# Transposes of q, k and the channel MLP's input: from TensorE to DMA transposes issued by ScalarE

## The chip, the core and the metric

The kernel runs on one core of a Trainium2 chip. The core has a matrix engine (TensorE, PE in the profile), VectorE (DVE), ScalarE (ACT), GpSimd (POOL) and SyncE (SP), each with its own in-order queue of instructions, and sixteen DMA engines that all queues share. A DMA is issued by an engine's queue (SPq, ACTq, POOLq in the profile) and lands later. The metric is device time in microseconds (us), the median over runs.

## The reference: what is computed

Eight batches of causal windowed attention, eight heads of 64 over 576 positions, feed an MLP mixer. Cut to what matters:

```python
# q, k, v: (8 batches, 8 heads, 576 positions, 64), float32
scores = q @ k.T / 8            # heads 0-3: 0 <= pos_q - pos_k < 32
                                # heads 4-7: 0 <= rel < 128 and rel % 4 == 0
x  = softmax(masked scores) @ v                  # -> (8, 576, 512)
h  = relu(x^T @ w_tok1) @ w_tok2                 # token MLP: 576 -> 256 -> 576
u  = x + h^T
out = u + relu(u @ w_ch1) @ w_ch2                # channel MLP: 512 -> 1536 -> 512
```

A matmul on TensorE contracts over the partition dimension. The scores contract over the 64 head channels and the channel MLP's first product over the 512 channels, while q, k and u arise with positions on the partitions. So q, k and u each have to be transposed once per batch: 576 positions by 512 channels, three times, eight batches.

## The kernel before

The 576 positions are handled as five strips (s_i) of 128, 128, 128, 128 and 64. Everything between the float32 loads and the float32 result is float16.

One batch goes through these steps. `emit_loads_dma` issues fifteen loads (q, k, v by strip; 128 partitions of eight 256-byte pieces) from SP. `gen_casts` turns them to float16: q on ScalarE, k and v on VectorE. `gen_attention` first transposes q and k: for q, then k, for each pair of heads hp, five TensorE transposes fill one PSUM tile `tp` (two buffers), and one VectorE copy moves it to `qt` or `kt` in SBUF (L184 to L203). Then for each head, `emit_qk` runs five score matmuls, two Exps on ScalarE and the mask product on GpSimd or VectorE; `emit_av` follows two or three heads later with ten matmuls, a reciprocal and a scaling product on VectorE that writes `xn`. `gen_mixer` runs the token MLP (h1p: ten matmuls, two Relus on ScalarE; up: ten matmuls, five VectorE adds that write `u16`), transposes u (L250 to L269: for each of four channel blocks cb, five TensorE transposes into `tp` and one VectorE copy to `uT`), then the channel MLP: gp (96 matmuls of 288 columns, Relus half on ScalarE and half on VectorE, giving twelve `gt`), and yp (sixty matmuls of 512 columns, five VectorE adds, five stores issued from SP).

Three streams are interleaved by `drive`: in iteration `it` the attention of batch `it`, the mixer of batch `it`-1 and the casts of batch `it`+1. Each generator yields a cost (C_TP, C_QK and so on) and the stream that has least progress goes next. A tile framework then places the instructions on the engines' queues and adds the semaphore waits; it may set an instruction earlier or later than it was traced. Every buffer has a fixed number of copies (`bufs`), so a writer waits until the readers of the copy before are done.

Each DMA issued from SP or ACT signals one of eight completion semaphores (DMAHW0 to DMAHW7), used in turn; a DMA that takes a semaphore again first waits until the DMA that used it before has landed. In the kernel before, all 163 such DMAs are SP's. The weights are loaded from GpSimd's queue, cast on the way.

## Time and profile before

| | |
|---|---|
| median of 3 runs | 401.49 us (400.77 to 402.12) |
| span of the profiled execution | 403.1 us; no other time is given for that execution |
| PE busy | 356.7 us, 89% of the span, 2784 matmuls |
| DVE, ACT, POOL busy | 228.7, 137.5, 101.9 us |
| PE on L190 (transposes of q, k) | 320 instructions, 34.55 us busy |
| PE on L255 and L261 (transposes of u) | 128 and 32 instructions, 15.62 and 6.34 us busy |
| DVE copies L197, L201, L267 | 32 each; 13.55, 15.48, 14.31 us busy |
| mean granted TensorE clock | 0.962 of full |

Matmuls are pipelined, and each row's duration includes a fixed part that overlaps with the next matmul. What a matmul costs TensorE is therefore the distance from its start to the start of the next one, not its busy time. The busy time of ACT leaves out what its queue spends on issuing DMAs; those have rows of their own, with the engine named ACTq.

### The profile page before, as it was taken

The page shows a single profiled execution, that of the slowest core. Times are in us where ns is not written, and L with a number is a line of the kernel's source. Part 1 is how long each engine was busy: PE and PEld are TensorE (multiplying, and loading weights), DVE is VectorE, ACT ScalarE, POOL GpSimd, SP SyncE. Part 2 cuts the span into 40 slices and gives each one's busy share as a digit, 9 for nine tenths or more (in the row PEclk, how much of TensorE's full clock was granted, in tenths as well). Part 3 has the DMA queues.
Part 4 walks back from the last instruction along what each step waited for, and adds up shares of the span by engine and source line. Part 5 has one row for each costly group of instructions (what it writes and reads, how often), then busy time and mean ns, then how long its engine had stood idle before and what let it go on. Part 6 is the DMA issues. An engine that isn't in the chain of part 4 may idle for free.

```text
span 403.1 us, 6967 instructions
## 1 busy us (share of the span) xinstructions
PE 356.7 (89%) x2784; PEld 218.3 (54%) x2784; DVE 228.7 (57%) x550; ACT 137.5 (34%) x281; POOL 101.9 (25%) x69
## 2 busy tenths in 40 slices
PE   0487659997899989999899989998999989996995
PEld 0254337553575547655675557654764557553752
DVE  2487437755885496638754586448543574445432
ACT  2164024443174325422462236331443206321310
POOL 0044301541062404260063205140235106240000
PEclk9999869996899999999899999999999989999899
DMA  9999999349933789486961250020002100020002
GB/s 192 210 214 218 199 198 221 86 112 215 198 77 78 184 180 208 71 210 155 171 122 52 67 91 2 28 78 15 2 0 80 41 0 2 26 80 14 2 38 81
DMA packets 121473, 42.50 MB, mean 105 GB/s; under 512 B 113696, under 2 KB 116064, under 8 KB 121440
## 3 DMA queue, kind: packets, MB, share of 16 engines
q1 hardware_dynamic: 118192, 38.32, 46.3%
q0 software_dynamic: 3248, 3.74, 5.3%
q8 instruction: 22, 0.36, 0.4%
q14 instruction: 11, 0.09, 0.1%
HBM read 36.34 MB, written 9.44 MB: 114 GB/s over the span
## 4 chain that ended last, share of the span: by engine, by line
PE 75%; DVE 13%; DMA 7%; SPq 2%; ACT 1%; issue 1%; POOL 1%; POOLq 0%; ACTq 0%
DMA l_k_3_138<-in_k_dram 6%; SPq L105 2%; DMA l_q_4_83<-in_q_dram 1%; PE yp_4_4709 L293 1%; PE yp_4_4133 L293 1%; PE yp_4_2282 L293 1%; PE yp_4_1665 L293 1%; PE yp_4_3516 L293 1%; PE yp_4_2899 L293 1%; PE yp_3_4669 L293 1%; PE yp_3_4092 L293 1%; PE yp_3_3475 L293 1%; PE yp_3_2241 L293 1%; PE yp_2_918 L293 1%; PE yp_1_877 L293 1%
## 5 line engine op out<-in xcount | busy, mean ns | idle before, releaser
L276 PEld LDWEIGHTS <-w_2_340 128*128 128x128 f16 x192 | 19.5, 102 | 9.9 <-issue 4.7
L276 PEld LDWEIGHTS <-w_0_321 128*128 128x128 f16 x192 | 18.5, 99 | 7.3 <-DVE xn_1159 L179 0.3
L276 PEld LDWEIGHTS <-w_3_357 128*128 128x128 f16 x192 | 19.5, 101 | 5.3
L276 PEld LDWEIGHTS <-w_1_337 128*128 128x128 f16 x192 | 18.9, 101 | 4.2
L190 PE MATMUL tp_q_0_149<-ident,q_0_97 128*128 128x128 f16 (+1 forms) x5 | 1.4, 275 | 14.5 <-ACT q_0_97 L118 14.5
L190 PEld LDWEIGHTS <-q_0_97 128*128 128x128 f16 (+1 forms) x20 | 1.6, 117 | 16.6 <-ACT q_0_97 L118 15.6
L155 POOL TENSOR_TENSOR att_0_792<-att_0_792,mask_63 128x1024 f16<-128x1024 f16 x1 | 2.1, 2116 | 22.0 <-ACT att_0_792 L152 22.0
L155 POOL TENSOR_TENSOR att_0_2548<-att_0_2548,mask_63 128x1024 f16<-128x1024 f16 x1 | 2.1, 2128 | 20.5 <-ACT att_0_2548 L152 20.5
L155 POOL TENSOR_TENSOR att_0_4369<-att_0_4369,mask_63 128x1024 f16<-128x1024 f16 x1 | 2.1, 2120 | 20.5 <-ACT att_0_4369 L152 20.5
L155 POOL TENSOR_TENSOR att_0_1314<-att_0_1314,mask_63 128x1024 f16<-128x1024 f16 x1 | 2.1, 2122 | 19.6 <-ACT att_0_1314 L152 19.6
L155 POOL TENSOR_TENSOR att_0_3165<-att_0_3165,mask_63 128x1024 f16<-128x1024 f16 x1 | 2.1, 2128 | 19.1 <-ACT att_0_3165 L152 19.1
L155 POOL TENSOR_TENSOR att_0_3782<-att_0_3782,mask_63 128x1024 f16<-128x1024 f16 x1 | 2.1, 2124 | 19.1 <-ACT att_0_3782 L152 19.1
L155 POOL TENSOR_TENSOR att_0_1931<-att_0_1931,mask_63 128x1024 f16<-128x1024 f16 x1 | 2.1, 2123 | 19.1 <-ACT att_0_1931 L152 19.1
L346 POOL DMA_DIRECT2D w_0_235<-in_moe_w_tok_dram x1 | 0.7, 720 | 24.5 <-DVE w_1_238 L340 24.5
L237 PEld LDWEIGHTS <-w_0_290 128*128 128x128 f16 x40 | 4.0, 100 | 4.7 <-issue 0.8
L237 PEld LDWEIGHTS <-w_1_304 128*128 128x128 f16 x40 | 3.9, 97 | 3.9
L222 PEld LDWEIGHTS <-w_1_238 128*128 128x128 f16 x16 | 1.7, 105 | 5.9 <-issue 5.2
L276 PE MATMUL gp_0_0_600<-uT_2_589,w_2_340 128*128 128x288 f16 x1 | 0.4, 399 | 4.4 <-DVE uT_2_589 L267 4.4
L155 POOL TENSOR_TENSOR att_4_1535<-att_4_1535,mask_65 128x1024 f16<-128x1024 f16 x1 | 2.1, 2120 | 8.5 <-ACT att_4_1535 L152 8.5
L155 POOL TENSOR_TENSOR att_4_2769<-att_4_2769,mask_65 128x1024 f16<-128x1024 f16 x1 | 2.1, 2123 | 8.2 <-ACT att_4_2769 L152 8.2
L155 POOL TENSOR_TENSOR att_4_4003<-att_4_4003,mask_65 128x1024 f16<-128x1024 f16 x1 | 2.1, 2123 | 8.2 <-ACT att_4_4003 L152 8.2
L155 POOL TENSOR_TENSOR att_4_4585<-att_4_4585,mask_65 128x1024 f16<-128x1024 f16 x1 | 2.1, 2117 | 8.2 <-ACT att_4_4585 L152 8.2
(3217 smaller groups left out, 1288.7 us busy)
## 6 DMA issues: line engine op xcount, KB each, us to landing
w_0_321<-in_moe_w_ch_dram POOLq DMA_DIRECT2D x1, 384.0 KB, 7.8
w_1_337<-in_moe_w_ch_dram POOLq DMA_DIRECT2D x1, 384.0 KB, 9.0
w_2_340<-in_moe_w_ch_dram POOLq DMA_DIRECT2D x1, 384.0 KB, 10.1
w_3_357<-in_moe_w_ch_dram POOLq DMA_DIRECT2D x1, 384.0 KB, 11.1
mask_63<-att_masks SPq DMA_DIRECT2D x1, 256.0 KB, 2.5
mask_65<-att_masks SPq DMA_DIRECT2D x1, 256.0 KB, 3.2
l_q_0_67<-in_q_dram SPq DMA_DIRECT2D x1, 256.0 KB, 3.9
l_k_0_69<-in_k_dram SPq DMA_DIRECT2D x1, 256.0 KB, 4.6
```

What stands on the lines that cost most here:

```text
L105: nc.sync.dma_start(out=t32[0:ns], in_=src[b, :, s0:s0 + ns, :].rearrange("h s d -> s h d"))
L155: eng.tensor_tensor(out=att, in0=att, in1=m, op=ALU.mult)
L190: nc.tensor.transpose(out=pst[:, 128 * s_i:128 * s_i + ns], in_=src[0:ns, s_i, 2 * hp:2 * hp + 2, :].rearrange("s h d -> s (h d)"), identi ...
L222: nc.tensor.matmul(out=p, lhsT=w1[s_i][:, 128 * jb:128 * (jb + 1)], rhs=xnb[:, s_i].rearrange("s h d -> s (h d)"), start=(s_i == 0), stop= ...
L237: nc.tensor.matmul(out=p, lhsT=w2[jb][:, s0:s0 + 128], rhs=h1[jb], start=(jb == 0), stop=(jb == 1),)
L276: nc.tensor.matmul(out=p[:, 0:288], lhsT=w3[cb][:, 128 * mb:128 * (mb + 1)], rhs=uT[cb][:, 288 * sh:288 * (sh + 1)], start=(cb == 0), stop ...
L293: nc.tensor.matmul(out=p, lhsT=gt[mb][:, s0:s0 + 128], rhs=w4[mb], start=(mb == 0), stop=(mb == 11),)
L346: nc.gpsimd.dma_start(out=t, in_=moe_w_tok1[128 * s_i:128 * (s_i + 1), :])
```

## The change: what it does

The 480 transposes on TensorE and the 96 copies out of PSUM are taken out, with the identity matrix and its load. In their place stand 120 DMA transposes, 15 per batch, issued from ScalarE's queue: five for q, five for k and five for u, one per strip. Each reads a strip of up to 128 positions by 512 channels in SBUF and writes all four transposed blocks at once, into one tile per batch of 128 x 4 x 640 (q, k) or 128 x 4 x 576 (u), each with two copies. In the built program each is one instruction that cuts its source into tiles of 16 rows by 128 columns. The cost that `drive` counts for the transposes of one attention goes from eight to five C_TP; the mixer's yields come as one.

```diff
 def gen_attention(b):
-        for nm in ("q", "k"):
-            for hp in range(4):
-                pst = ps.tile([128, 1024], FP16, tag="tp", bufs=2, name=f"tp_{nm}_{b}_{hp}")
-                for s_i in range(NSB):
-                    ns = SB[s_i] if nm == "q" else 128
-                    src = q16 if nm == "q" else k16
-                    nc.tensor.transpose(
-                        out=pst[:, 128 * s_i:128 * s_i + ns],
-                        in_=src[0:ns, s_i, 2 * hp:2 * hp + 2, :].rearrange("s h d -> s (h d)"),
-                        identity=ident[0:ns, 0:ns],
-                    )
-                if nm == "q":
-                    qt = sb.tile([128, S], FP16, tag="qt", bufs=8, name=f"qt_{b}_{hp}")
-                    nc.vector.tensor_copy(out=qt, in_=pst[:, 0:S])
...
-                yield C_TP
+        qt = sb.tile([128, 4, KTW], FP16, tag="qt", bufs=2, name=f"qt_{b}")
+        kt = sb.tile([128, 4, KTW], FP16, tag="kt", bufs=2, name=f"kt_{b}")
+        for s_i in range(NSB):
+            ns = SB[s_i]
+            s0 = 128 * s_i
+            nc.scalar.dma_start_transpose(
+                out=qt[:, :, s0:s0 + ns],
+                in_=q16[0:ns, s_i].rearrange("s h d -> s (h d)"))
+            nc.scalar.dma_start_transpose(
+                out=kt[:, :, s0:s0 + 128],
+                in_=k16[:, s_i].rearrange("s h d -> s (h d)"))
+            yield C_TP
+        for hp in range(4):
+            qt_tiles[(b, hp)] = qt[:, hp]
+            kt_tiles[(b, hp)] = kt[:, hp]
 def gen_mixer(b):
-        uT = []
-        for cb in range(4):
-            pst = ps.tile([128, 1024], FP16, tag="tp", bufs=2, name=f"tpu_{b}_{cb}")
-            for s_i in range(NSB):
...
-            t = sb.tile([128, S], FP16, tag="ut", bufs=8, name=f"uT_{b}_{cb}")
-            nc.vector.tensor_copy(out=t, in_=pst[:, 0:S])
-            uT.append(t)
-            yield C_UT
+        uTt = sb.tile([128, 4, S], FP16, tag="ut", bufs=2, name=f"uT_{b}")
+        for s_i in range(NSB):
+            if s_i < 4:
+                nc.scalar.dma_start_transpose(out=uTt[:, :, 128 * s_i:128 * s_i + 128], in_=u16[s_i])
+            else:
+                nc.scalar.dma_start_transpose(out=uTt[:, :, 512:576], in_=u16[s_i][64:128])
+        yield 4 * C_UT
+        uT = [uTt[:, cb] for cb in range(4)]
...
-    nc.sync.dma_start(out=ident, in_=ident_dram)
...
-            n_att = 8 * C_TP + 8 * C_QK + 8 * C_AV
+            n_att = 5 * C_TP + 8 * C_QK + 8 * C_AV
```

Where the new instructions come to stand on ScalarE's queue is decided by the framework. Two places matter. In the rows below, names are the program's with the batch left out (att_7 is the masked score tile of head 7, h_4_0 the first half of the token MLP's hidden layer of batch 4, qt the transposed q), L numbers are lines of each kernel's own file, and the brackets name the semaphores that are waited for.

The first place is ScalarE's queue at the end of batch 4's attention. Before, the last Exp of head 7 is followed by the two Relus of the token MLP:

```order
L152 ACTIVATE att_7_2895<-scB_7_2889 128x512 [waits PE_49]
L229 ACTIVATE h_4_0_3000<-h1p_0_2994 128x512 [waits PE_49]
L229 ACTIVATE h_4_1_3008<-h1p_1_3002 128x512 [waits PE_49]
L118 CAST q_7_3912<-l_q_0_3581 128x512 [waits DMAHW3_49,PE_49]
L118 CAST q_7_3912<-l_q_1_3587 128x512 [waits DMAHW6_49]
L283 ACTIVATE gt_0_3124<-gp_0_0_3125 128x288 [waits PE_49]
```

Now ten transposes stand between them:

```order
L152 ACTIVATE att_7_2529<-scB_7_2523 128x512 [waits PE_49]
L189 DMA_TRANSPOSE qt_3184<-q_6_2862 128x4x128 [waits DMAHW4_49]
L192 DMA_TRANSPOSE kt_3185<-k_6_2863 128x4x128 [waits DMAHW5_49]
L189 DMA_TRANSPOSE qt_3184<-q_6_2862 128x4x128 [waits DMAHW7_49]
L192 DMA_TRANSPOSE kt_3185<-k_6_2863 128x4x128
L189 DMA_TRANSPOSE qt_3184<-q_6_2862 128x4x128 [waits DMAHW1_49]
L192 DMA_TRANSPOSE kt_3185<-k_6_2863 128x4x128 [waits DMAHW2_49]
L189 DMA_TRANSPOSE qt_3184<-q_6_2862 128x4x128 [waits DMAHW3_49]
L192 DMA_TRANSPOSE kt_3185<-k_6_2863 128x4x128 [waits DMAHW5_49]
L189 DMA_TRANSPOSE qt_3184<-q_6_2862 128x4x64 [waits DMAHW6_49]
L192 DMA_TRANSPOSE kt_3185<-k_6_2863 128x4x128 [waits DMAHW7_49]
L224 ACTIVATE h_4_0_2634<-h1p_0_2628 128x512 [waits PE_49]
```

They are batch 6's, which become possible when batch 4's scores have freed the tile's copy; batch 4's Relu is queued behind them. The same stands before the Relus of batches 3 (ten) and 5 (ten), and seven stand before batch 2's; before batch 0's stand four of batch 1, before batch 1's two, and before those of batches 6 and 7 none. The eighth of the ten takes the semaphore of the second again (DMAHW5), and the tenth that of the third (DMAHW7).

The second place follows on the same queue: from the token MLP's Relus to the first Relu of the channel MLP. The five transposes of u now stand there, each waiting for one VectorE add:

```order
L224 ACTIVATE h_4_1_2642<-h1p_1_2636 128x512 [waits PE_49]
L248 DMA_TRANSPOSE uT_2682<-u_4_0_2652 128x4x128 [waits DMAHW0_49,DVE_49]
L151 ACTIVATE att_0_2695<-scA_0_2688 128x512 [waits PE_49,Pool_49]
L248 DMA_TRANSPOSE uT_2682<-u_4_1_2659 128x4x128 [waits DMAHW1_49,DVE_49]
L248 DMA_TRANSPOSE uT_2682<-u_4_2_2666 128x4x128 [waits DMAHW2_49,DVE_49]
L248 DMA_TRANSPOSE uT_2682<-u_4_3_2671 128x4x128 [waits DMAHW3_49,DVE_49]
L152 ACTIVATE att_0_2695<-scB_0_2689 128x512 [waits PE_49]
L250 DMA_TRANSPOSE uT_2682<-u_4_4_2678 128x4x64 [waits DMAHW4_49,DVE_49]
L266 ACTIVATE gt_0_2699<-gp_0_0_2700 128x288 [waits PE_49]
```

On TensorE, what stood between up and the third block of gp was forty of the transposes; now only one head's scores stand there, and gp follows directly.

## The prediction

> **What bounds the kernel now.** I read the page's busy lines first, then busy time by stage, then the order of time in one steady batch.

> ```profile
> PE 356.7 (89%) x2784; PEld 218.3 (54%) x2784; DVE 228.7 (57%) x550; ACT 137.5 (34%) x281; POOL 101.9 (25%) x69
> PE 75%; DVE 13%; DMA 7%; SPq 2%; ACT 1%; issue 1%; POOL 1%; POOLq 0%; ACTq 0%
> 20.00:30.00 10.00, 8.45 (x69) 5.62 (x67) 8.35 (x37) 6.12 (x13) 4.70 (x9) 1.00 1.36 214
> 40.00:60.00 20.00, 12.48 (x69) 6.86 (x67) 7.62 (x16) 3.59 (x8) 3.17 (x6) 0.74 1.11 196
> 240.00:260.00 20.00, 20.00 (x182) 14.14 (x181) 11.98 (x31) 9.42 (x22) 6.37 (x3) 1.00 0.01 2
> ```

> The columns of the last three rows are PE, PEld, DVE, ACT, POOL, the granted clock, the DMA share and GB/s. Until about 60 us the loads and weights hold the DMA engines (a share over 1, 214 GB/s). After that TensorE holds the time: the chain of waits is 75% PE. ScalarE is a third busy, which looks like room for DMA issues. But an average says little about an in-order queue; what counts is the stretch between two batches, where the chain leaves TensorE. ScalarE, VectorE and TensorE there, in order of time (start, duration, what; in brackets the idle time before it):

> ```profile
> 226.63 0.59 ACT L152 ACTIVATE att_7_2895<-scB_7_2889 128x512 f16<-128x512 f32 x1
> 232.99 0.60 ACT L229 ACTIVATE h_4_0_3000<-h1p_0_2994 128x512 f16<-128x512 f32 x1 [5.77 <-PE h1p_0_2994 L222]
> 235.13 0.69 DVE L244 TENSOR_TENSOR u_4_0_3022<-up_0_3019,xn_2393 128x512 f16<-128x512 f32 x1 [0.26 <-PE up_0_3019 L237]
> 235.74 0.68 DVE L244 TENSOR_TENSOR u_4_1_3035<-up_1_3032,xn_2393 128x512 f16<-128x512 f32 x1
> 237.90 0.68 DVE L244 TENSOR_TENSOR u_4_4_3066<-up_4_3063,xn_2393 128x512 f16<-128x512 f32 x1
> 241.39 0.44 PE L190 MATMUL tp_k_2_3116<-ident,k_5_2679 128*128 128x128 f16 x5
> 241.67 0.29 PE L276 MATMUL gp_0_0_3125<-uT_2_3106,w_2_340 128*128 128x288 f16 x1
> 243.94 0.30 PE L276 MATMUL gp_2_0_3170<-uT_0_3082,w_0_321 128*128 128x288 f16 x1
> 244.07 0.29 PE L276 MATMUL gp_2_0_3170<-uT_1_3098,w_1_337 128*128 128x288 f16 x1
> 244.19 0.29 PE L276 MATMUL gp_2_0_3170<-uT_2_3106,w_2_340 128*128 128x288 f16 x1
> ```

> The reader is to see three things. ScalarE has 5.77 us free before the Relu of h1p. From the first add of u to the third gp block are 243.94 - 235.13 = 8.81 us, in which u is transposed and two gp blocks run. And five transposes occupy TensorE from 241.39 to 241.67, 0.056 us each, though their rows count for more.

> **What is removed.** Sixty transposes per batch at 0.056 are 3.4 us of TensorE, 27 us in eight batches. That is all there is to win on the engine, and it is not won whole: forty of the sixty lie inside the 8.81 us, which are weighed below as one piece. The other twenty are q's, ahead of the token MLP. There the gain is a stall and a delayed product:

> ```profile
> 231.25 0.52 PE L190 MATMUL tp_q_2_3037<-ident,q_5_2678 128*128 128x128 f16 x5 [0.60 <-DVE qt_0_3017 L197]
> 230.78 0.42 DVE L197 COPY qt_0_3017<-tp_q_0_3011 128x576 f16<-128x576 f16 x1
> 231.12 0.48 DVE L179 TENSOR_TENSOR xn_2393<-av_7_2943,rec_7_2953 128x320 f16<-128x320 f32 x1
> ```

> The copy keeps the last xn product back by 231.12 - 230.78 = 0.34 us, and five q transposes (0.28) stand among the up matmuls: I take 0.6 per batch for seven batches, **-4 us**. The 96 copies free VectorE (57% busy), which ends no wait in the gp and yp stages; nothing for those.

> **What is added: the price of one issue.** No DMA transpose is in the trace. ScalarE's queue is held while it issues one; call that T. The nearest rows are SP's issues (start, duration):

> ```profile
> 0.74 0.33 SPq L323 DMA_DIRECT2D ident<-ident  x1
> 2.07 0.50 SPq L105 DMA_DIRECT2D l_q_0_67<-in_q_dram  x1
> 3.23 1.36 SPq L105 DMA_DIRECT2D l_q_1_71<-in_q_dram  x1
> 5.64 1.32 SPq L105 DMA_DIRECT2D l_q_2_75<-in_q_dram  x1
> 8.08 1.32 SPq L105 DMA_DIRECT2D l_q_3_79<-in_q_dram  x1
> 31.29 9.75 SPq L105 DMA_DIRECT2D l_k_3_138<-in_k_dram  x1
> out_dram<-o_0_1_890 SPq DMA_DIRECT2D x1, 256.0 KB, 2.0
> l_q_2_130<-in_q_dram SPq DMA_DIRECT2D x1, 256.0 KB, 5.9
> ```

> From below 0.33 us: 128 rows, nothing queued. From above 1.36 where loads of 1024 pieces follow back to back (9.75 once, beside the weight loads). A transpose of a strip reads 512 pieces of 256 bytes, but writes rows of 16 elements, 4096 of them, and ten or five follow each other. It is nearest to the back-to-back loads: T = 1.3 us. [...] The landing after the issue I take from the quickest DMA, 2.0 less its own issue of about 0.4: 1.6 us; the loads' 5.9 is its upper end.

> **Ten transposes ahead of the Relu.** One of the ten is half a strip, so they hold the queue for 9.7 T = 12.6 us. 5.77 of it is covered by ScalarE's idle time; 6.8 us delay the Relu, and behind it up, u and gp. Three batches (3, 4, 5) have that; batch 2 has seven, 9.1 us, against a cover of 2.71:

> ```profile
> 144.03 0.60 ACT L229 ACTIVATE h_2_0_1766<-h1p_0_1760 128x512 f16<-128x512 f32 x1 [2.71 <-PE h1p_0_1760 L222]
> ```

> Together 3 x 6.8 + 6.4 = **+27 us**. At T = 0.33 it is nothing (3.2 under 5.77). Also queued behind the ten is nothing else that is due; VectorE and TensorE wait for the Relu alone. The other q and k transposes of batches 1 to 3 lie among the gp Relus, where ScalarE is half idle (9.42 of 20 us): nothing, and up to their issue time if the Relus' PSUM tiles run out.

> The eight completion semaphores, now shared by SP and ScalarE, add waits on both queues. The eighth of the ten waits for the second's landing, six issues (7.8 us) earlier: nothing, unless a landing takes that long. SP's loads may wait behind a transpose's landing; they run more than a batch ahead (the DMA share from 240 to 260 us is 0.01), so nothing, except in the first 60 us, where a late load is a late batch and would come on top of the start's term below. GpSimd's queue is not passed.

> **The five transposes of u.** After the first add (0.69) the queue issues five, one of them half, and two Exps (0.49 each apart): 0.69 + 4.7 T + 1.0, then 1.6 to land, then two gp blocks of eight matmuls at 0.12 (243.94 to 244.07 to 244.19), 1.95: 5.2 + 4.7 T, at T = 1.3 11.35 us against 8.81. That is 2.5 us for each of eight batches, **+20 us**. TensorE has only one head's scores to do meanwhile.

> **The start.** Batch 0's and 1's twenty transposes fall into the stretch where the DMA engines are full. 128 KB at the 214 GB/s of that stretch are 0.61 us, nineteen strips' worth: **+12 us**; nothing if they fit into gaps.

> **The clock.** When TensorE waits some us, it resumes slowly. At the last batch it does so already:

> ```profile
> 370.76 0.20 PE L261 MATMUL tpu_0_4805<-ident,u_7_4_4803 64*128 64x64 f16 x1 [0.31 <-DVE u_7_4_4803 L244]
> 371.90:376.00 4.10, 4.10 (x23) 2.63 (x24) 1.37 (x3) 0.82 (x2) 0.00 (x0) 0.58 0.02 4
> ```

> At a granted 0.58 those 4.1 us hold 1.7 us of loss. The steady batches run at 1.00. New waits of over 6 us come at the u transposes of six more batches and at four Relus: ten times 1.7, **+17 us** (nothing, if the waits stay short).

> The sum is 403.1 - 4 + 27 + 20 + 12 + 17 = 475 us of span. The median of the runs is 0.996 of the span before (401.49 / 403.1): **473 us**, slower by 18%.

> **The rivals.** *Issues are cheap.* At T = 0.5, the uncontended load, the ten need 4.9 us and hide under 5.77, and the u chain follows VectorE's pace: the fifth add ends 5 x 0.6 + 0.1 after the first began, then 0.35 + 1.6 + 1.95, 7.0 us against 8.81: -1.8 in eight batches, -14. With -4 and +12 at the start it gives 397 us of span, 395; with a start that hides, 384. For it speaks that issues with nothing queued are this short; against it that none here is short once several follow each other. [...]

> *The DMA path, not the issue, is the bound.* If one strip takes as long as a loaded landing, about 5 us, and they follow one after the other, fifteen need 75 us per batch against the 43.8 that a batch takes now (gp_2 of batch 4 at 243.94, of batch 5 at 287.76 below). It decides from 2.9 us per strip. Eight batches then take 403 + 8 x 31 = 653 us. For it speaks the count of small writes; against it that loads of twice the bytes were issued every 1.3 us.

> ```profile
> 287.76 0.60 PE gp_2_0_3787 L276 x4
> ```

> [...]

> *An issue twice as dear.* At T = 2.2 the Relus wait 3 x 15.6 + 12.7 = 59 us and the u chain 8 x 6.7 = 54: 403 - 4 + 59 + 54 + 12 + 17 = 541, 539 us. Nothing in the rows excludes it between 1.36 and 9.75.

> **How the numbers follow.** Chances: the forecast (T from 0.9 to 1.8; 435 to 510 us) 0.45, the dearer issue (510 to 590) 0.2, the bound path (over 590) 0.17, cheap issues 0.18, of which 0.11 end faster, 0.03 level and 0.04 slower. A difference of 0.3%, about 1.2 us, is what can be told from no change. So faster 0.11, the same 0.03, slower 0.86. The range 405 to 600 leaves out most of the cheap case and the worst of the bound path; the forecast's own range is 435 to 510.

> **What would show it.** Issue rows of L189, L192, L248 on ACTq near 1.3 us; before the Relus of batches 3 to 5, ten in a row with TensorE waiting for ScalarE; from the first u add to the third gp block some 11 us; a granted clock below 1 after both. The forecast is wrong if ACTq's rows are under 0.6 us, if the transposes land long after the issue, or if ScalarE idles while TensorE waits for DMA.

## The result, and the profile after

The changed kernel takes 473.77 us (median of 4 runs, 470.42 to 475.62), the kernel before beside it 401.81 us: a ratio of 1.177, 95% interval 1.172 to 1.182. The profiled span is 471.1 us against 403.1, the mean granted clock 0.875 against 0.962. First the page of the changed kernel: busy time, the clock by slices, the chain of waits by engine, and one group.

```profile
PE 333.8 (71%) x2304; PEld 191.0 (41%) x2304; DVE 187.7 (40%) x454; ACT 138.6 (29%) x281; POOL 102.2 (22%) x69
PEclk9999858996799957996679986999779997999599
PE 57%; ACTq 14%; DMA 13%; DVE 9%; issue 3%; ACT 2%; POOL 1%; SPq 0%; DVEq 0%; POOLq 0%
L259 PE MATMUL gp<-uT,w 128*128 128x288 f16 x768 | 119.5, 317 | 57.5 <-DMA uT<-u 56.0
```

TensorE has 480 instructions and 23 us of busy time less, VectorE 41 us less, and the end comes 68 us later. ScalarE's busy share fell to 29%, and yet its queue (ACTq, 0% of the chain before) now carries 14% of the chain: issuing is not counted as busy. TensorE waits 56.0 us for the landing of uT. Here is what one issue costs (duration in ns, least, median, most):

```profile
L189 ACTq DMA_TRANSPOSE qt<-q x40: 1186/1241/2132, 6.6 to 331.9; - x40
L192 ACTq DMA_TRANSPOSE kt<-k x40: 1204/1262/6134, 7.9 to 333.2; - x40
L248 ACTq DMA_TRANSPOSE uT<-u x32: 1204/1230/1368, 59.4 to 435.8; - x32
L250 ACTq DMA_TRANSPOSE uT<-u x8: 1185/1199/1267, 66.2 to 437.2; - x8
```

And the stretch between two batches that the prediction took apart, batch 4, ScalarE in order of time:

```profile
266.26 2.13 ACTq L189 DMA_TRANSPOSE qt<-q  x1
268.43 1.29 ACTq L192 DMA_TRANSPOSE kt<-k  x1
269.76 1.29 ACTq L189 DMA_TRANSPOSE qt<-q  x1
...
279.06 1.28 ACTq L192 DMA_TRANSPOSE kt<-k  x1
280.39 1.09 ACT L224 ACTIVATE h<-h1p 128x512 f16<-128x512 f32 x2 [13.27 <-DMA qt<-q]
```

TensorE in the same stretch:

```profile
271.35 2.32 PE L217 MATMUL h1p<-xn,w 128*128 128x512 f16 x10 [1.61 <-DVE xn L179]
281.04 4.24 PE L232 MATMUL up<-h,w 128*128 128x512 f16 x10 [7.37 <-ACT h L224]
289.65 1.12 PE L259 MATMUL gp<-uT,w 128*128 128x288 f16 x4 [3.84 <-DMA uT<-u]
292.27 3.04 PE L259 MATMUL gp<-uT,w 128*128 128x288 f16 x12 [1.50 <-DMA uT<-u]
295.79 2.13 PE L259 MATMUL gp<-uT,w 128*128 128x288 f16 x16
```

The ten issues hold the Relu back until 280.39. TensorE stands for 7.37 us; then ten up matmuls take 4.24 us where the ten of h1p, of the same size, took 2.32, and twelve gp matmuls take 3.04 us where sixteen take 2.13 a little later. The clock granted over these four groups is 0.54 (up) and 0.52 (the twelve), against 1.00 (h1p and the sixteen).

Where the 68 us lie, by stage, from the first or last row of each stage in the two traces (us; difference of after to before, summed over the eight batches):

| stage | sum | batches with most of it |
|---|---|---|
| start up to the first h1p matmul | +9.5 | 0 |
| h1p to the first Relu | +30.3 | 0: 3.5; 2: 3.0; 3: 9.2; 4: 7.8; 5: 6.9 |
| Relu to the first add of u | +3.7 | 1, 3, 4, 5: 0.8 to 1.1 each |
| first add of u to the first yp matmul | +29.6 | 0: 0.2; 2: 7.2; the others 2.6 to 4.9 |
| yp and the last add of o | -4.5 | seven batches, 0.64 each |
| last add of o to the next batch's h1p | -0.7 | 1: +0.6; most others -0.25 |

The rows add up to 68 us, where the medians are 72 apart, mostly because the profiled execution of the kernel before is a long one: its span is 403.1 us at a mean clock of 0.962, and seventeen others of it, run beside `late`, have a median span of 400.4 us at 0.970.

### The profile page after: what moved, and what is told of

It reads as the page before. It is cut to its first block, busy times and chain, and to the rows that moved or that the text cites. A ratio compares the mean times of both kernels' runs of the same rounds, so it can differ in the third digit from the quotient of the medians.

```text
span 471.1 us, 6129 instructions
## 1 busy us (share of the span) xinstructions
PE 333.8 (71%) x2304; PEld 191.0 (41%) x2304; DVE 187.7 (40%) x454; ACT 138.6 (29%) x281; POOL 102.2 (22%) x69
## 3 DMA queue, kind: packets, MB, share of 16 engines
q10 hardware_dynamic: 61184, 14.70, 18.9%
## 4 chain that ended last, share of the span: by engine, by line
PE 57%; ACTq 14%; DMA 13%; DVE 9%; issue 3%; ACT 2%; POOL 1%; SPq 0%; DVEq 0%; POOLq 0%
PE gp L259 23%; PE yp L276 21%; ACTq L192 6%; DMA uT<-u 5%; DMA l_k<-in_k_dram 4%; ACTq L189 4%; PE scA L143 4%; ACTq L248 4%; DVE u L239 4%; PE up L232 3%; PE scB L143 2%; DMA kt<-k 2%; PE h1p L217 2%; PE av L165 2%; DMA qt<-q 2%
## 5 line engine op out<-in xcount | busy, mean ns | idle before, releaser
L259 PE MATMUL gp<-uT,w 128*128 128x288 f16 x768 | 119.5, 317 | 57.5 <-DMA uT<-u 56.0
L155 POOL TENSOR_TENSOR att<-att,mask 128x1024 f16<-128x1024 f16 x42 | 89.2, 2125 | 277.3 <-ACT att L152 270.2
L259 PEld LDWEIGHTS <-w 128*128 128x128 f16 x768 | 77.9, 106 | 90.3 <-issue 33.4
L276 PE MATMUL yp<-w,gt 128*128 128x512 f16 x480 | 109.8, 380 | 0.0
L268 DVE TENSOR_SCALAR gt<-gp 128x288 f16<-128x288 f32 x96 | 43.7, 456 | 94.4 <-PE gp L259 94.0
L151 ACT ACTIVATE att<-scA 128x512 f16<-128x512 f32 x64 | 38.2, 598 | 105.0 <-PE scA L143 76.9
L276 PEld LDWEIGHTS <-gt 128*128 128x128 f16 x480 | 44.2, 98 | 51.1
L266 ACT ACTIVATE gt<-gp 128x288 f16<-128x288 f32 x96 | 39.5, 412 | 71.8 <-PE gp L259 59.9
L232 PE MATMUL up<-h,w 128*128 128x512 f16 x80 | 27.9, 516 | 28.2 <-ACT h L224 28.2
L152 ACT ACTIVATE att<-scB 128x512 f16<-128x512 f32 x64 | 37.8, 596 | 24.2 <-DMA uT<-u 12.2
L143 PE MATMUL scA<-qt,kt 64*128 64x256 f16 x128 | 27.4, 303 | 18.5 <-DMA qt<-q 18.5
L118 ACT CAST q<-l_q 128x512 f16<-128x512 f32 (+1 forms) x40 | 24.5, 615 | 53.9 <-DMA qt<-q 13.7
L179 DVE TENSOR_TENSOR xn<-av,rec 128x320 f16<-128x320 f32 x64 | 30.6, 489 | 1.4
L121 DVE CAST k<-l_k 128x512 f16<-128x512 f32 (+1 forms) x40 | 20.3, 507 | 24.5 <-DMA l_k<-in_k_dram 24.4
L232 PEld LDWEIGHTS <-w 128*128 128x128 f16 x80 | 9.9, 124 | 44.9 <-issue 40.6
## 6 DMA issues: line engine op xcount, KB each, us to landing
l_q<-in_q_dram SPq DMA_DIRECT2D x32, 256.0 KB, 5.0
l_k<-in_k_dram SPq DMA_DIRECT2D x32, 256.0 KB, 4.1
l_v<-in_v_dram SPq DMA_DIRECT2D x32, 256.0 KB, 4.9
out_dram<-o SPq DMA_DIRECT2D x32, 256.0 KB, 2.2
```

Of the source, the lines that this page charges most:

```text
L143: nc.tensor.matmul(out=sc[:, co:co + nq], lhsT=kt[r:r + 64, 128 * kb:128 * kb + 128], rhs=qt[r:r + 64, q0:q0 + nq], start=True, stop=True,)
L151: nc.scalar.activation(out=att[:, 0:512], in_=scA, func=AF.Exp, scale=0.125)
L152: nc.scalar.activation(out=att[:, 512:1024], in_=scB, func=AF.Exp, scale=0.125)
L155: eng.tensor_tensor(out=att, in0=att, in1=m, op=ALU.mult)
L232: nc.tensor.matmul(out=p, lhsT=w2[jb][:, s0:s0 + 128], rhs=h1[jb], start=(jb == 0), stop=(jb == 1),)
L259: nc.tensor.matmul(out=p[:, 0:288], lhsT=w3[cb][:, 128 * mb:128 * (mb + 1)], rhs=uT[cb][:, 288 * sh:288 * (sh + 1)], start=(cb == 0), stop ...
```

## The experiments

Each run differs from the changed kernel by the edit shown, if not said otherwise; times are medians, with the kernel before run beside it (401.7 to 404.0 us).

**One part undone at a time.** `u_back` transposes u on TensorE again (lines 250 to 269 of the kernel before in place of this), `qk_back` q and k (lines 184 to 203, and 8 C_TP again):

```diff
-                nc.scalar.dma_start_transpose(out=uTt[:, :, 128 * s_i:128 * s_i + 128], in_=u16[s_i])
+                    nc.tensor.transpose(
+                        out=pst[:, 128 * s_i:128 * s_i + 128],
+                        in_=u16[s_i][:, 128 * cb:128 * (cb + 1)],
+                        identity=ident,
+                    )
```

> The transposes of u are back on TensorE with their copies; q and k stay DMA transposes. Theory (each issue holds ScalarE's queue for about 1.2 us; the loss is the Relu that waits behind ten of them, the chain of five before gp, the start, and the halved clock after each wait): what the two profiles put between the first u add and yp (29.6 us over eight batches) goes, and the k transposes stay out of that stretch (another 1 us per batch), while start (9.5) and Relu waits (30) stay: about 436 us. Rival (the DMA path's own throughput is the bound, so the loss goes with the number of strips transposed): two thirds of the loss stay, about 450 us.

> The transposes of q and k are back on TensorE; u stays DMA transposes. Theory: start and Relu waits go, the u chain stays at 3 to 4 us per batch with its cold clock: about 428 us. Rival (throughput of the DMA path): one third of the loss, about 426 us, so this run alone does not tell them apart; the theory's parts should add up with those of the run that puts u back (34 + 26 against 72 in all, the rest being k and q transposes that are away in both).

`u_back` took 440.81 us (437.76 to 444.57), `qk_back` 437.35 us (435.48 to 437.95). So u's DMA transposes are worth 33 us, those of q and k 36, and the two add up (69 of 72). The first is near the theory's 436; the second is 9 us above its 428. By stage both are clean: in `u_back` the first add of u to yp is back at the kernel before (-2.3 us) and the Relus still cost 31; in `qk_back` only the former is left (+30.0). The waits of TensorE (us in total, times, longest), first in the changed kernel, then in `u_back`:

```profile
PE gp L259 <- DMA uT<-u: 56.0, 15, 11.5
PE up L232 <- ACT h L224: 28.2, 6, 8.8
```

```profile
PE up L232 <- ACT h L224: 28.7, 6, 7.7
```

**The same transposes, issued earlier on the same queue.** `behind_exps` puts two transposes behind each of the Exps of heads 3 to 7 of the batch before, from batch 2 on, so that no ten stand in a row ahead of the Relu:

```diff
+            with (tc.issue_after(exp_mark[(b - 1, 3 + s_i)]) if b >= 2 else nullcontext()):
                 nc.scalar.dma_start_transpose(
                     out=qt[:, :, s0:s0 + ns],
```

> The same instructions on the same queue; only the order is changed: from batch 2 on, the two transposes of a strip are issued behind the Exp of head 3 to 7 of the batch before, where ScalarE has idle time in the yp stage, and not ten in a row ahead of the Relu. Theory: the Relu waits of batches 2 to 5 go: about 442 us. Rival (number or traffic of the transposes is what costs): 473 us, unchanged.

446.63 us (445.54 to 448.1), near the theory's 442 and far from 473. The stage from h1p to the Relu costs 5.1 us more than before instead of 30.3, 3.8 of it in batch 0, where nothing was moved:

```profile
PE gp L262 <- DMA uT<-u: 60.9, 16, 11.0
PE up L235 <- ACT h L227: 3.3, 2, 2.3
```

It is the place in the in-order queue, not the transfer, that q's and k's transposes cost here: same engine, same DMAs, 27 us less.

**Another queue.** `from_sp` issues all fifteen from SP; the line for u, and likewise those for q and k:

```diff
-                nc.scalar.dma_start_transpose(out=uTt[:, :, 128 * s_i:128 * s_i + 128], in_=u16[s_i])
+                nc.sync.dma_start_transpose(out=uTt[:, :, 128 * s_i:128 * s_i + 128], in_=u16[s_i])
```

> The same 120 transposes, issued from SyncE's queue instead of ScalarE's. Theory (ScalarE's queue is what is held): the Relu waits of batches 2 to 5 and the slow up matmuls after them go (31 us), and the two Exps no longer stand among the five transposes of u (up to 8 us): 435 us, more if the u transposes wait behind loads on SP. Rival (the DMA path or the landing is what is waited for): the same 473 us.

500.79 us (499.57 to 503.18): both missed, by 66 and 28 us. The Relus do come on time (h1p to Relu -0.6), so the reading of ScalarE's queue holds; but the rest costs more than was saved. SP's queue in its trace, from the last store of one batch on:

```profile
247.12 0.53 SPq L287 DMA_DIRECT2D out_dram<-o  x1
247.74 2.07 SPq L189 DMA_TRANSPOSE qt<-q  x1
249.86 1.25 SPq L192 DMA_TRANSPOSE kt<-k  x1
...
260.30 1.26 SPq L192 DMA_TRANSPOSE kt<-k  x1
261.61 0.58 SPq L105 DMA_DIRECT2D l_q<-in_q_dram  x1
262.30 5.13 SPq L248 DMA_TRANSPOSE uT<-u  x4
```

The ten stand behind a store that waits for the yp stage to end, and u's five behind the ten. The chain of waits runs through the store, nine of the ten, a landing and u's issues. The largest single part lies elsewhere: batch 0 is 41 of the 95 us by which this trace is longer than that of the kernel before, 25 of them ahead of its first h1p matmul. There the ten stand behind the loads of batches 0 and 1, and the first is issued at 34.85 us. An issue costs 1.25 to 1.27 us here too: the price is not ScalarE's.

**Fewer issues.** `merged` transposes four strips at once and the last one by itself, four issues per batch for q and k instead of ten; the score matmuls read the new layout, and one of a head's five is split in two:

```diff
+        nc.scalar.dma_start_transpose(
+            out=qt[:, 0:4].rearrange("p s c r -> p (s c) r"),
+            in_=q16[:, 0:4].rearrange("p s h d -> p (s h d)"))
```

> The five q and five k transposes of a batch become two and two: one transposes strips 0 to 3 at once (128 rows x 2048 columns, sixteen blocks of 128x128), one the last strip. The bytes moved and the engine that issues are the same. Theory, from the half strip of u at 1.199 us beside the full strip at 1.230 us in the changed kernel: the price of an issue is nearly fixed, so four issues take 4 x 1.25 = 5 us in place of 12.5 us, the first transfer of 16 blocks lands later, and the Relu waits ahead of the up matmuls of batches 2 to 5 (27 us) and batch 0 (3 us) mostly go: 473 - 27 = about 446 us. The u transposes keep their cost. Rival: the price goes by the number of blocks (4 a strip), a merged issue costs about 4 x 1.25 = 5 us, and nothing is won: about 473 us.

456.38 us (452.98 to 458.91): between the two, 10 us above the theory. The Relu stage costs 8.3 us more than before instead of 30.3. The issues, in ns:

```profile
L191 ACTq DMA_TRANSPOSE qt<-q x8: 1413/2650/3520, 13.7 to 307.9; - x8
L194 ACTq DMA_TRANSPOSE kt<-k x8: 1877/3160/5732, 15.3 to 310.9; - x8
L198 ACTq DMA_TRANSPOSE qt<-q x8: 1185/1233/1807, 21.8 to 313.5; - x8
```

An issue of four times the size costs 2.65 and 3.16 us, not 1.25 and not 5; the first of all, with nothing before it, 1.41. So a price per instruction is most of it for a strip, but not all of it for a large one. The rest speaks for a queue that fills rather than for a price per block: the two shortest of q's (1.41 and 1.51 us) are followed at once by the two longest of k's (5.73 and 4.40 us), which have as many blocks. That wasn't tried by itself.

**The start.** `start_on_pe` transposes q and k of batches 0 and 1 on TensorE, by the code of before (its first and last statement are shown):

```diff
+        if b < 2:
+            for nm in ("q", "k"):
...
+                        kt_tiles[(b, hp)] = kt
+                    yield C_TP
+        else:
```

> q and k of batches 0 and 1 are transposed on TensorE and copied by VectorE as in the kernel before; q and k of batches 2 to 7 and all of u stay DMA transposes from ScalarE's queue. Theory: the start (9.5 us up to the first token MLP matmul, and 3.5 us between it and the first Relu of batch 0) is the price of the transposes of the first two batches, so both go: 473 - 13 = about 460 us. Rival: the start is longer because the transposes' packets slow the first loads through the DMA engines of all batches, or the time comes back as a wait in batch 1 or 2: 470 us or more.

465.01 us (461.71 to 466.3). The start is 0.5 us over the kernel before instead of 9.5, and batch 0's Relu waits no more: those 13 us are the transposes of the first two batches, as the theory has it. Some came back: the u stage (first add of u to yp) of batch 0 is 2.7 us longer than in the changed kernel, batch 2's Relu waits 3.5 us longer, and 9 of the 13 are left.

**The clock.** `kept_busy` adds matmuls of 512 columns into a PSUM tile that nothing reads, where TensorE waits:

```diff
+        if 2 <= b <= 5:
+            with tc.issue_after(last_h1.ins):
+                for i in range(26):
+                    nc.tensor.matmul(out=warm, lhsT=w3[0][:, 0:128], rhs=w4[0], start=True, stop=True)
```

and fourteen more behind up in batches 1 to 7; `kept_busy_2` has 30, 36, 22, 17, 17, 17 and 22 there.

> The changed kernel with matmuls of 128x128 by 128x512 into a PSUM tile that nothing reads, put on TensorE where it waits: 26 behind the token MLP's first product in batches 2 to 5, and 14 behind its second product in batches 1 to 7. No DMA, wait or order of the other work is changed. Theory: after each wait of 6 to 12 us the next 3 to 5 us of matmuls run at half the granted clock (0.42 us in place of 0.22 for 512 columns, 0.25 in place of 0.13 for 288), which is about 1 us for the up matmuls of batches 1 to 5 and 1.5 to 2 us for the gp matmuls of seven batches, 14 to 16 us in all; with TensorE kept busy the clock stays up and this goes: about 458 us, with a mean clock above 0.95. Rival: the first matmuls after a wait are slow for another reason, or the added matmuls hold up the ones that are wanted: 473 us or more.

> As the run before it, with more of the unread matmuls behind the token MLP's second product: 30, 36 and 22 in batches 1 to 3, 17 in 4 to 6, 22 in 7, in place of 14. There TensorE still stood 4.7 us (batch 1), 5.3 (2) and 2.6 (3) ahead of the first gp matmul, and those gp matmuls ran at half the clock again. Theory (the slow matmuls after a wait are the clock's): with the waits filled the gp matmuls of batches 1 to 3 and 7 run at 0.13 us too, 1 to 2 us each, so 4 to 6 us below the run with 14, whose profiled span was 461 us: a span of about 456 us, and the group of gp matmuls near 107 us busy in place of 111.7. Rival (they are slow for another reason, such as operands that arrive late): gp stays at 111 to 112 us busy, and the added matmuls push the time up to 465 us or more.

468.72 us (462.71 to 473.21) and 473.52 us (470.78 to 474.68); in the profiled executions, the quickest of each, the clock rose to 0.939 and 0.972. The groups of up and gp in the changed kernel, in `kept_busy` and in `kept_busy_2` (the first number behind the bar is busy us):

```profile
L259 PE MATMUL gp<-uT,w 128*128 128x288 f16 x768 | 119.5, 317 | 57.5 <-DMA uT<-u 56.0 <-ACT gt L266 1.5
L232 PE MATMUL up<-h,w 128*128 128x512 f16 x80 | 27.9, 516 | 28.2 <-ACT h L224 28.2
```

```profile
L267 PE MATMUL gp<-uT,w 128*128 128x288 f16 x768 | 111.7, 303 | 42.2 <-DMA uT<-u 42.1
L236 PE MATMUL up<-h,w 128*128 128x512 f16 x80 | 22.0, 422 | 6.8 <-ACT h L224 6.5
```

```profile
L267 PE MATMUL gp<-uT,w 128*128 128x288 f16 x768 | 107.8, 296 | 30.3 <-DMA uT<-u 30.1
L236 PE MATMUL up<-h,w 128*128 128x512 f16 x80 | 23.0, 435 | 9.0 <-ACT h L224 8.8
```

The slow matmuls are the clock's: with TensorE kept busy the two groups lose 13.7 and 16.6 us, as the theory says. The time follows in part, and both runs miss their forecasts. The first's four runs (462.71, 467.14, 470.31, 473.21 us) spread widely and lie 1 to 11 us below the changed kernel's median, the two quicker ones 9 on average; the second's median is the changed kernel's. The profiles say where the time is won, counting each batch to its last add of o. Batches 4 to 7, by which all loads have landed (the last at 266.9 us in the changed kernel), take 187.5 us in both instead of 197.9. Of these 10.4 us, 7.2 are won between the first add of u and yp, where these batches are still 7.2 over the kernel before. Batches 0 to 3 take 269.9 us in the first and 278.0 in the second, against 269.6. In `kept_busy_2` the Relu of batch 2 and the adds of u of batches 2 and 3 come 2 to 4 us later than without the added matmuls. VectorE there, batch 2:

```profile
170.25 0.43 DVE L121 CAST k<-l_k 128x512 f16<-128x512 f32 x1 [5.22 <-DMA l_k<-in_k_dram]
174.13 0.27 DVE L123 MEMSET k<- 64x256 uint32 x1 [3.46 <-DMA kt<-k]
174.43 3.08 DVE L243 TENSOR_TENSOR u<-up,xn 128x512 f16<-128x512 f32 x5
```

The adds of u stand behind a cast that waits for a load and a memset that waits for a transpose. So in these batches a faster TensorE meets a later VectorE. Why the loads are this late there, and so what the clock is worth beside the loads, stays open.

**A version that keeps what is good.** `mixed` leaves u, and q and k of batches 0 and 1, on TensorE, and issues the rest behind the Exps. `late` does the same with q and k of batches 5 to 7 alone; the two lines by which it differs from `mixed`:

```diff
-        if b < 2:
+        if b < 5:
...
-            n_att = 5 * C_TP + 8 * C_QK + 8 * C_AV
+            n_att = (8 if it < 5 else 5) * C_TP + 8 * C_QK + 8 * C_AV
```

`late_order` is the control: the kernel before with the order's number of `late`,

```diff
-            n_att = 8 * C_TP + 8 * C_QK + 8 * C_AV
+            n_att = (8 if it < 5 else 5) * C_TP + 8 * C_QK + 8 * C_AV
```

> u and the q and k of batches 0 and 1 are transposed on TensorE as in the kernel before; only q and k of batches 2 to 7 are DMA transposes from ScalarE's queue, and two of them at a time stand behind each of the Exps of heads 3 to 7 of the batch before, not in a row ahead of the Relu. Theory: nothing waits for them there, and what the change was worth without its waits is left: in the run with the u transposes back on TensorE the stages from the Relu to the gp matmuls took 2.3 us less than before, and those of the channel MLP's second half 4.5 us less, over eight batches; six batches of this are about 5 us, so 396 us, 390 to 400. Rival: the transposes among the Exps delay the scores of the next heads on ScalarE by 1.25 us each, and this reaches TensorE: 402 us or more, up to 402 + 6 x 5 = 432 us.

> The kernel before in batches 0 to 4; in batches 5 to 7, when the loads from memory are nearly done, q and k are transposed by DMA from ScalarE's queue behind the Exps of the batch before; u stays on TensorE throughout. Theory from the run with both means mixed from batch 2 on, whose batches 5, 6 and 7 took 1.9, 2.1 and 2.2 us less than in the kernel before, and whose loss was all in batches 1 to 4, beside the loads: 402 - 6 = about 396 us, 394 to 398. Rival: the win in those batches is only the order of the work, which gives it back elsewhere, or batch 7's share (it has no transposes of q and k beside it) does not come again: 400 to 403 us, no difference that can be measured.

> The kernel before with one number of the order changed: from the fifth round of its outer loop on the attention's planned length counts five transpose steps in place of eight, as in the run with DMA transposes in batches 5 to 7 alone. No DMA transposes. Theory (the 0.7% of that run is the TensorE transposes and VectorE copies of q and k that left): no difference to the kernel before, 401 to 403 us. Rival (it is the order): 399 to 400 us, as that run.

> The run with DMA transposes of q and k in batches 5 to 7 once more, on the same chip as its control. If its gain stands: 399 to 400 us, 2 to 4 us below the kernel before; if it was chance, 401 us or more.

`mixed` took 408.42 us, 1.016 of before (1.013 to 1.020): a miss, 12 us above the theory. Its batches 5 to 7 are 5.6 us shorter than before (batch 7 by 1.6, not the 2.2 that the next expectation has), its batches 1 to 4 are 10.6 longer. In batch 1 VectorE's queue stands again behind a transpose:

```profile
104.44 0.27 DVE L124 MEMSET k<- 64x256 uint32 x1 [7.02 <-DMA kt<-k]
105.09 3.08 DVE L264 TENSOR_TENSOR u<-up,xn 128x512 f16<-128x512 f32 x5
```

The time lies in the rival's range, but not by the rival's way: TensorE waits 4.4 us in all for Exps and masked scores, against 2.5 in the kernel before. `mixed` also counts five C_TP in every round, so part of its loss may be the order's, which the control below shows to cost something in `late`; for `mixed` this wasn't tried.

`late` took 399.35 us, 0.993 of before (0.990 to 0.996), and 399.11 us, 0.993 (0.990 to 0.995), when measured again beside its control (six runs, five of 397.3 to 399.25 us and one of 1141.66): faster than both kernels, by 3 us, half of what was expected. Part of the missing half is batch 4, whose u stage got 2.0 us longer. In both its profiles the u stages of batches 1 and 3, which the edit doesn't touch, are 1.5 us shorter. That is the clock, which was granted at 0.93 and 0.92 over these two stages in the profile of the kernel before and at 1.00 in those of `late`; here is batch 3 in the kernel before, then in `late` (the third number from the end is the clock):

```profile
189.92:212.49 22.57, 21.37 (x185) 15.36 (x183) 15.47 (x36) 11.51 (x25) 6.37 (x3) 0.92 0.82 147
```

```profile
189.39:210.49 21.10, 19.90 (x184) 14.51 (x183) 15.45 (x36) 10.81 (x23) 6.37 (x3) 1.00 0.88 164
```

So 2.9 of the 5.4 us by which the two spans differ are the clock's, in stages whose instructions are the same. The 1.6 us of batch 7, in `mixed` as in `late`, also come with a clock of 0.91 before and 1.00 after; whether the edit brings that about isn't shown. The control took 406.18 us, 1.012 (1.008 to 1.016): the order alone costs 4 us, so the gain isn't the order's, though the order had been held for neutral. Against its own order `late` wins 7 us.

## Why the prediction was right, and where its terms were not

The time forecast was 473, measured 473.77; the sum was 475 of span, measured 471.1. The mechanism of the large terms is right: an in-order queue held by issues at 1.3 us each, TensorE behind it. That the sum comes so close is partly luck, since it is closer than its terms are.

**The price of an issue.** T = 1.3 us was taken from SP's back-to-back loads. Measured: 1.20 to 1.26 us a row, 1.33 from start to start (nine issues from 268.43 to the Relu at 280.39). Right. The choice rested on the nearest row, and the cheap-issue rival (0.5) and the dearer one (2.2) both fall with it. The half strip, counted as half, is not: 1.199 us against 1.230 for the full one, 0.03 us less for half the rows.

**Landing.** Forecast 1.6 us after the issue, the loaded landing of 5.9 as the upper end. In batch 4 the landing of the last strip comes 2.38 us after the start of its issue, 1.2 after its end (the chain of waits of the changed kernel):

```profile
283.37 3.09 DVE u L239 x5
...
289.75 2.38 DMA uT<-u
...
292.27 3.04 PE gp L259 x12
```

Beside the loads it takes longer. The last strips of batches 2 and 3 in the same chain:

```profile
172.34 4.22 DMA uT<-u
...
231.97 4.79 DMA uT<-u
```

The bound-path rival, which needed 2.9 us a strip, falls: issues follow each other every 1.3 us without slowing down, and the last five of batch 4's ten land 2.4 to 2.5 us after their starts, the first five 2.5 to 4.6. The small writes that spoke for it were counted from the program's tiles and aren't shown: the trace has 61,184 packets and 14.70 MB on the queue of the 120 transposes (q10 on the page), 510 packets an issue.

**Ten ahead of the Relu: +27.** Measured 26.8 us in batches 2 to 5, the mechanism confirmed by `behind_exps`. Inside, two errors cancel. Batches 3 to 5 cost 23.8, not 20.4, since the first of the ten takes 2.13 us and the half strip a full price (14.1 us for ten, not 12.6); batch 2 costs 3.0, not 6.4: its seven begin at 153.72 us, 5.0 us ahead of h1p and 9.35 ahead of the Relu, so that 6.3 us of them are covered and not 2.71. Not forecast is batch 0's 3.5 us, which are one issue beside the loads:

```profile
45.91 6.13 ACTq L192 DMA_TRANSPOSE kt<-k  x1
52.09 0.60 ACT L224 ACTIVATE h<-h1p 128x512 f16<-128x512 f32 x1 [7.51 <-issue]
```

The prediction had such a row in hand, a load's issue of 9.75 us beside the weight loads, and used it for the dearer-issue rival only.

**The u chain +20, and the clock +17.** Together 37; measured 33.3 (29.6 and 3.7). In batch 4 the last strip lands 8.8 us after the first add of u, against 9.4 forecast, and the third gp block starts 12.4 after it (283.37 to 295.79), against 11.35, the difference being gp matmuls at half the clock (0.50 over the first four, 0.52 over the next twelve). The clock's size, too, holds as time on TensorE: the up group is 7.9 us busier than in `qk_back` (27.9 against 20.0), the gp group 10.6 busier than in `u_back` (119.5 against 108.9), 18.5 us in all. As a term of the sum it is shown for batches 4 to 7 alone. Five or six of the ten waits that the prediction counted lie there, 8.5 to 10.2 us at 1.7 each, and the two runs that keep TensorE busy win 10.4; the u stage is then 1.8 us longer than before in each of these batches, against 2.5 forecast. In batches 0 to 3, beside the loads, the two runs win nothing, so the other waits aren't shown to cost what was added for them. The rows that the term was read from don't show its condition either: ahead of them, in batch 7 of the kernel before, TensorE stands 1.61 us before h1p and then at most 0.52 us at a time, not some us.

```profile
L264 PE MATMUL gp<-uT,w 128*128 128x288 f16 x768 | 119.6, 312 | 36.9 <-DMA uT<-u 36.9
L237 PE MATMUL up<-h,w 128*128 128x512 f16 x80 | 20.0, 380 | 0.0
```

```profile
L271 PE MATMUL gp<-uT,w 128*128 128x288 f16 x768 | 108.9, 297 | 8.0 <-DVE uT L262 7.0 <-ACT gt L278 1.0
```

(The two fences are groups of `qk_back` and of `u_back`.)

**The loads after 60 us, the shared completion semaphores, and the transposes among the gp Relus: nothing.** The last of the three holds: TensorE's gp matmuls wait 1.5 us in all for ScalarE's Relus. The first failed. The prediction called the loads a batch ahead after 60 us, from a window at 240; from 60 to 220 us the DMA engines are 0.73 busy already in the kernel before and full in the changed one (the kernel before first; the DMA share is the column before the last):

```profile
60.00:220.00 160.00, 152.93 (x1241) 95.15 (x1239) 104.02 (x240) 64.91 (x135) 46.90 (x22) 0.96 0.73 147
```

```profile
60.00:220.00 160.00, 121.32 (x854) 70.16 (x855) 72.75 (x171) 54.35 (x111) 38.32 (x18) 0.84 0.97 178
```

What this costs can be read from the landings above: 4.22 and 4.79 us in batches 2 and 3 against 2.38. The u stage of batch 2 is 3.6 us longer than that of batch 4; 1.8 are the landing, 0.5 a transpose of q that stands ahead of u's on the queue, and 1.3 pass on TensorE after the landing.

The semaphores do add waits: SP's loads wait for transposes to land, 96 us in all in the changed kernel (SP's waits: us, times, longest), where all SP's waits for a DMA are 1.6 us in the kernel before:

```profile
SPq L105 <- DMA qt<-q: 35.8, 12, 5.2
SPq L105 <- DMA kt<-k: 30.4, 8, 19.1
SPq L105 <- DMA uT<-u: 29.7, 9, 7.3
```

What these waits cost in time isn't shown. VectorE's casts of k wait 24.4 us for their loads, about 16 in the kernel before, and all but some 4 of the 24.4 lie before 66 us. That it is the shared semaphore, and not the DMA engines' order, that ties a load to a transpose is read from the program and wasn't tried alone.

**The start: +12.** Measured 9.5, and 3.5 more at batch 0's Relu; `start_on_pe` shows that these are the transposes. The way to the number isn't shown: it was the bytes of nineteen strips, but batch 1's first four are issued from 41.4 us on and h1p starts at 46.32, and up to there the chain of waits passes through three landings of batch 0's (5.57, 2.62 and 5.85 us). That 12 is near 9.5 is luck as far as this goes.

**What the removal wins: -4, and VectorE's copies nothing.** Ahead of h1p it is 0.25 us a batch, not 0.6. The 0.64 us that seven yp stages got shorter were not forecast; the control `late_order` has 0.65 in batches 4 to 6 without any DMA transpose, so it is work that the order moved elsewhere, not a gain of VectorE's.

## What to carry to other kernels

An engine that is 29% busy can still be the bound: ask what its in-order queue holds at the moment when the others wait for it, count each DMA issue there at its full price (1.2 to 1.3 us), and move the issues behind work that isn't waited for before choosing another queue; another queue brings what it is itself waiting for (here the first won 27 us, the second lost 27). Ask when the loads are really done, from windows over the whole span and not from one: beside them a transpose lands in 4 to 5 us instead of 2.4. Here the transposes of q and k behind the Exps lost 1.6% when they began in batch 2, beside the loads, and won 0.7% in the last three batches; how much of the loss is the order's wasn't tried. Before a difference between two profiles is put down to an edit, compare the granted clock of the stages that the edit doesn't touch. A sum that comes out within 1% can hold terms that are wrong, so test the terms, not the sum.
